# A causal mask moved from TensorE into masked copies for 12 of 32 head pairs, a smaller ring of x, and a new plan

## The chip, the cores and the metric

The kernel runs on one core of a Trainium2 chip. The core has a matrix engine (TensorE, PE in the profile, with its weight loads as PEld), a vector engine (VectorE, DVE), a scalar engine (ScalarE, ACT), GpSimd (POOL) and a sync engine that issues DMAs (SyncE, SP). Each engine runs its own instructions in the order in which they were issued, and they meet through semaphores. The metric is the time of one execution on the device in microseconds; less is better. A time is the median of several runs.

## The reference

A forgetting attention is followed by a SwiGLU block. There are 8 batches of 8 heads with 576 positions of width 64; the model width is 512, the inner width 1536, and 8 x 576 = 4608 tokens go through the second part.

```python
scores = scale * np.matmul(q, k.transpose(0, 1, 3, 2))
cum = np.cumsum(np.log(np.clip(f, 0.0001, 1.0)), axis=-1)
decay = cum[:, :, :, None] - cum[:, :, None, :]
causal = np.triu(np.ones((S, S), dtype=bool), k=1)
scores = np.where(causal, -1000000000.0, scores + decay)
attn = softmax(scores)            # rows, with 1e-9 added to the sum
x = np.matmul(attn, v)            # heads laid side by side: 4608 x 512
g = x @ w_gate
out = (g * sigmoid(g) * (x @ w_val)) @ w_out
```

Within a row of scores the term of the row's own position is the same for every column, so the softmax needs only the gate sums `cum` of the columns.

## The kernel before

**Attention.** Two heads of one batch make a pair, so there are 32 pairs. A row block `i` is 64 positions of both heads (128 partitions) and has 64(i+1) columns. Blocks 0 to 3 are group 0 of a pair, blocks 4 to 8 group 1; each group is a unit, named `a<pair>.<group>` in the table of nudges. For a block TensorE multiplies q (`qz`, negated and scaled) by k (`kt`) into a score bank `sp` (L594). VectorE adds the gate sums `cb` and takes the least value of each row in the same instruction (`tensor_tensor_reduce`, L622; it gives `t` and the least value `tm`). ScalarE takes the exponential and the row's sum (L642). VectorE makes the reciprocals (`lr`, L658 and L660), GpSimd scales the rows into bf16 (`pk`, L678), and the result is transposed into `pT`: on TensorE with a copy by VectorE or ScalarE for pairs 0 to 7 (L708, L713), by a DMA from SyncE's queue (L691) for the rest. TensorE multiplies `pT` by v (`vt`) into a bank `tx` (L734), which is copied into `xT` (L758).

**The mask.** Because the scores are negated, a masked position must be large. In the kernel before, each block's diagonal 64 columns get a second matmul, identity times a 64-column mask, added into the same bank (L598), for every pair below `MFROM`, which is 32: all of them. The other way is in the code but unused. There a copy of a pair's gate sums with the mask added to every 64-column stretch (`copies`, tile `cm`) is used for the diagonal columns, a block is split into a body that adds `cb` and a diagonal that adds `cm`, both parts give their own least value, and a tiny GpSimd instruction (`least`) takes the smaller of the two before the exponential.

**Feed-forward.** `xT` is a ring of `NRING` tokens. For each token tile (`TILES`: 256, 256, seven of 512, 256, 128, 128) TensorE makes gate and value into `gv` banks (L816), ScalarE a tanh (L822), VectorE the products (L824, L827, giving `hh`). TensorE then multiplies by the third weight (L844), and the copy `ot` is stored. This work fills TensorE between pieces of attention.

**What sets the order.** The program describes each operation with its engines, estimated durations, tiles and a priority, and a planner (`Plan.order`) simulates the engines and emits each engine's instructions in the order of its simulated start times. Among operations that could start at the same time the lower priority number goes first. `NUDGE` adds a number to the priority of a unit (`a` attention, `q` its inputs, `v` the cast of v, `f` a feed-forward tile, `o` its output). `STARTUP` is the order of the first loads: `p` is k and q of a pair (first halves for pairs 0 to 3), `k` and `q` the second halves, `c` a pair's gate sums, `v` v, `wg`, `wv`, `wo` weight pieces, `f9` the gates f. Each load in this line is planned behind the one `AHEAD` places before, and a weight load, which GpSimd issues, also behind the one `BEHIND` places before. The gate sums are computed once, stored to a DRAM tensor (L382) and loaded back for each pair, spread over 64 partitions (L513, L430).

Of the kernel before, what the change touches and what calls it, by code (L numbers as in the profile page):

```python
# [8 lines left out]
F32 = mybir.dt.float32  # L9
# [23 lines left out]
class Plan:  # L33
# [29 lines left out]
    def order(self):  # L63
# [72 lines left out]
        while ready:  # L136
# [63 lines left out]
def kernel(  # L200
# [28 lines left out]
    NRING = 2560  # L229
# [10 lines left out]
    MFROM = 32  # L240
# [15 lines left out]
    BEHIND = 6  # L256
# [4 lines left out]
    SLACK = 400  # L261
# [3 lines left out]
    STARTUP = "p0 f9 k0 p2 wv0 wg0 c0 v01 q1 q0 wv2 wg2 c1 v02 v00 k2 v04 c3 q2 wv4 v03 wg4 q3 c2 p4 v11 c4 wg8 wv8 c5 v14 p5 v13 v12 p6 c7 v10 c6 wo0 wo4 wo8 p7"  # L265
# [3 lines left out]
    NUDGE = "a5.0:-2 a8.0:1 a13.0:-1 a15.0:-2 a17.0:-2 a18.0:1.5 a22.0:2.5 a23.0:-1 a25.1:-1 a26.1:-1.5 f1:-2 f5:9 f7:0.5 o3:-4.5 o4:-0.5 o6:-8 o7:-3 q8:-2 q13:-3.5 q20:-2 q23:2 q25:4 q26:3.5 q30:-2"  # L269
# [33 lines left out]
    bufs("t", [P, S], F32, 4)  # L303
    for i in range(0, NB, 2):
        bufs(f"e{i}", [P, QB * (i + 2)], F32, 2)
# [187 lines left out]
    def load_parts(p):  # L493
        b, hp = divmod(p, NPB)
        pl.key(("cb", p), "cb", p)
        for name, x, a, z, r, n in parts(p):
            fk = (name + "f", p, x)
            pl.key(fk, name + "f")
            m = (z - a) // r

            def load(e, fk=fk, src=(k if name == "k" else q), a=a, z=z, r=r, n=n, m=m):
                for u in range(n):
                    h0 = 2 * (hp + u)
                    (nc.scalar if e == "ACT" else nc.sync).dma_start(
                        out=pl.buf(fk)[m * u:m * u + m, :, 0:r * D],
                        in_=src[b, h0:h0 + 2, a:z].rearrange("h (p r) d -> p h (r d)", r=r))
            loads[name, p, x] = pl.op({"ACT" if p == 0 and x == "A" else "SP": 550 * n}, load, (), [fk], -99 + 3 * p, dma=n * (z - a) * 2)
# [367 lines left out]
    for x in STARTUP.split():  # L875
# [96 lines left out]
```

## Time and profile before

| | |
|---|---|
| median of 3 runs | 419.31 us (417.72 to 420.36) |
| span of the profiled execution | 417.2 us |
| DMA, mean over the span | 172 GB/s, 71.83 MB |
| mask matmuls (L598) | 288, mean 197 ns each, as the profile counts |
| weight loads of the identity for them | 288, mean 100 ns |
| mean granted TensorE clock | 0.996 |

A line of the profile names an engine, the source line, and the tiles it writes and reads. "Busy" counts overlapping instructions of one engine once; a matmul's duration reaches from its start to its modelled end, so matmuls that follow each other overlap. The chain of waits is read from the end backwards: each piece is there because the next one waited for it. In a windows view each row is a stretch of the span: its start and end, its length, then busy time and number of instructions for each engine, the granted clock, the DMA engines' busy share and GB/s. In a view of groups a row gives a line, engine, operation and shapes, the count, the busy time and the mean ns, and what the engine waited for before it.

### The profile page before, as it was taken

The numbers are of one execution on the slowest core, as the hardware profiler recorded it, in microseconds if no ns is written. First come the engines' busy times: TensorE is split into PE (matmuls) and PEld (weight loads), VectorE is DVE, ScalarE is ACT, GpSimd is POOL, SyncE is SP. The second block draws the span as 40 slices with busy tenths as digits, with TensorE's granted clock in tenths as the row PEclk, the third lists the DMA queues.
The fourth block names the chain that finished last, engine by engine and source line by source line (L and its number), as shares of the span: only waits on it lengthen the run. The fifth ranks groups of instructions, "written<-read, shape, count | busy, mean of one in ns | idle before, by whom it ended". The sixth has DMA issues, their size and how long they took to land.

```text
span 417.2 us, 9955 instructions
## 1 busy us (share of the span) xinstructions
PE 398.3 (95%) x3250; PEld 232.3 (56%) x3296; DVE 328.9 (79%) x1065; ACT 310.3 (74%) x872; POOL 251.7 (60%) x459
## 2 busy tenths in 40 slices
PE   1979999999999999999999999999999999999996
PEld 0636878665555555555555554555555444457675
DVE  5688999999998899989897797798967764565232
ACT  4798999989995999899999984798996533232221
POOL 7589698987887897976968678267773400000000
PEclk9998999999999999999999999999999999999999
DMA  9999979695999999899999999848999211000211
GB/s 183 253 210 225 190 135 252 159 234 141 200 229 215 264 218 236 203 232 222 228 234 218 240 221 223 194 116 190 221 217 186 55 37 50 25 27 25 77 52 52
DMA packets 144004, 71.83 MB, mean 172 GB/s; under 512 B 117904, under 2 KB 131728, under 8 KB 143952
## 3 DMA queue, kind: packets, MB, share of 16 engines
q1 hardware_dynamic: 137568, 65.95, 71.1%
q0 software_dynamic: 5808, 4.72, 7.6%
q10 hardware_dynamic: 576, 0.52, 0.5%
q8 instruction: 26, 0.43, 0.4%
q14 instruction: 26, 0.21, 0.3%
HBM read 46.65 MB, written 9.58 MB: 135 GB/s over the span
## 4 chain that ended last, share of the span: by engine, by line
PE 86%; DVE 4%; issue 1%; ACT 0%
PE gv L816 43%; PE gv L844 22%; PE sp L594 9%; PE tx L734 6%; PE tx L467 3%; PE sp L598 2%; PE gv L708 2%; DVE t L622 1%; DVE pT L713 1%; DVE hh L827 1%; DVE th L824 1%; DVE qz L481 1%; DVE kt L481 0%; ACT ot L851 0%; DVE tm L622 0%
## 5 line engine op out<-in xcount | busy, mean ns | idle before, releaser
L622 DVE CUSTOM_DVE_ANT_0 t<-sp,cb 128x320 f32<-128x320 f32 (+7 forms) x288 | 130.4, 475 | 12.1 <-PE sp L598 8.6
L678 POOL TENSOR_SCALAR pk<-e,lr 128x128 bf16<-128x128 f32 (+3 forms) x190 | 100.5, 533 | 61.8 <-DVE lr L660 16.5
L816 PE MATMUL gv<-xT,wg 128*128 128x512 bf16 (+2 forms) x563 | 110.6, 327 | 0.8
L816 PE MATMUL gv<-xT,wv 128*128 128x512 bf16 (+2 forms) x562 | 109.3, 324 | 0.9
L844 PE MATMUL gv<-wo,hh 128*128 128x512 bf16 (+1 forms) x425 | 104.2, 373 | 0.8
L824 DVE SCALAR_TENSOR_TENSOR th<-th,gv 128x512 f32<-128x512 f32 x108 | 73.9, 684 | 39.3 <-ACT th L822 38.3
L822 ACT ACTIVATE th<-gv 128x512 f32<-128x512 f32 x108 | 64.1, 594 | 44.0 <-PE gv L816 43.1
L642 ACT ACTIVATE e<-t,tm 128x576 f32<-128x576 f32 (+4 forms) x160 | 88.7, 556 | 8.9 <-DVE tm L622 8.3
L827 DVE TENSOR_TENSOR hh<-th,gv 128x512 bf16<-128x512 f32 x108 | 73.7, 685 | 8.7 <-PE gv L816 4.9
L642 ACT ACTIVATE eo<-t,tm 128x128 f32<-128x128 f32 (+3 forms) x128 | 71.1, 556 | 4.7 <-DVE tm L622 2.9
L594 PE MATMUL sp<-kt,qz 128*128 128x448 bf16 (+6 forms) x320 | 71.9, 293 | 1.5 <-DVE tm L622 1.4
L678 POOL TENSOR_SCALAR pk<-eo,lr 128x128 bf16<-128x128 f32 (+3 forms) x127 | 67.6, 532 | 5.4 <-DVE lr L660 3.1
L816 PEld LDWEIGHTS <-wg 128*128 128x128 bf16 x576 | 49.8, 98 | 35.7
L816 PEld LDWEIGHTS <-wv 128*128 128x128 bf16 x576 | 48.9, 98 | 33.7 <-issue 0.3
L844 PEld LDWEIGHTS <-hh 128*128 128x128 bf16 x444 | 39.9, 98 | 39.0
L598 PE MATMUL sp<-mask,ident 128*128 128x64 bf16 x288 | 48.0, 197 | 0.0
L594 PEld LDWEIGHTS <-qz 128*128 128x128 bf16 x320 | 30.9, 100 | 20.9 <-DVE tm L622 0.9
L851 ACT ACTIVATE ot<-gv 128x512 f32<-128x512 f32 (+1 forms) x31 | 17.9, 580 | 27.1 <-PE gv L844 26.2
L598 PEld LDWEIGHTS <-ident 128*128 128x128 bf16 x288 | 27.2, 100 | 12.6 <-issue 1.9
L734 PE MATMUL tx<-pT,vt 128*64 128x320 bf16 (+4 forms) x448 | 29.6, 266 | 1.9 <-DVE pT L713 1.3
L451 POOL TENSOR_SCALAR qb<-qf 72x1024 bf16<-72x1024 f32 x28 | 29.1, 1041 | 3.1 <-DMA qf<-in_q_dram 2.0
L642 ACT ACTIVATION_READ_ACCUMULATOR e<-t,tm 128x1 f32 x160 | 30.6, 192 | 0.0
(69 smaller groups left out, 389.0 us busy)
## 6 DMA issues: line engine op xcount, KB each, us to landing
out_dram<-ot SPq DMA_DIRECT2D x35, 256.0 KB
vf<-in_v_dram SPq DMA_DIRECT2D x32, 256.0 KB
cb<-cum_f SPq DMA_DIRECT2D x56, 144.0 KB
kf<-in_k_dram SPq DMA_DIRECT2D x28, 288.0 KB
qf<-in_q_dram SPq DMA_DIRECT2D x28, 288.0 KB
wo<-in_moe_w_out_dram POOLq DMA_DIRECT2D x3, 512.0 KB, 10.8
vf<-in_v_dram SPq DMA_DIRECT2D x8, 128.0 KB
wv<-in_moe_w_val_dram POOLq DMA_DIRECT2D x2, 512.0 KB, 8.4
```

The costliest lines, as they stand in the source:

```text
L451: eng[e].tensor_scalar(dst, src, -scale, 1.0, op0=ALU.mult, op1=ALU.mult)
L594: nc.tensor.matmul(sp[:, o:o + z - a], qz[:, i, :, :].rearrange("p h r -> p (h r)"), kt[:, a:z], start=True, stop=not last or p >= MFROM)
L598: nc.tensor.matmul(sp[:, o - QB:o], ident, mask, start=False, stop=True)
L622: nc.vector.tensor_tensor_reduce(out=pl.buf(tk)[:, a:z], in0=pl.buf(sk)[:, o:o + z - a], in1=pl.buf(("cm", p))[:, i, :] if own else pl.buf ...
L642: nc.scalar.activation(pl.buf(ek)[:, :L], pl.buf(tk)[:, :L], AF.Exp, bias=pl.buf(("tm", p, g))[:, 0, i:i + 1], scale=-1.0, accum_out=pl.bu ...
L678: eng[e].tensor_scalar(dst, src, r, 1.0, op0=ALU.mult, op1=ALU.mult)
L734: nc.tensor.matmul(xo[r, 0:QB * n], vt[:, c, 2 * hp + h, :], pT[:, a:a + n, 64 * h:64 * h + 64], start=(c == 0), stop=(c == nch - 1))
L816: nc.tensor.matmul(pl.buf(bk)[:, j * n:j * n + n], wt[:, ko, fc * P:fc * P + P], xT[:, ko, x0:x0 + n], start=ko == 0, stop=ko == KD - 1)
L822: pl.op({"ACT": 487}, lambda e, u=u: nc.scalar.activation(pl.buf(("th", t, u)), pl.buf(("wg", t, u)), AF.Tanh, scale=0.5), [("wg", t, u)], ...
L824: pl.op({"DVE": 605}, lambda e, u=u: nc.vector.scalar_tensor_tensor(pl.buf(("th", t, u)), pl.buf(("th", t, u)), 1.0, pl.buf(("wg", t, u)), ...
L827: pl.op({"DVE": 605}, lambda e, u=u: nc.vector.tensor_mul(pl.buf(("hh", t, u)), pl.buf(("th", t, u)), pl.buf(("wv", t, u))), [("u", t, u), ...
L844: nc.tensor.matmul(pl.buf(bk)[:, 0:z - a], hh[:, (fc % nf) * n + ms * P:(fc % nf) * n + ms * P + P], wo[:, fc, a:z], start=fc == 0, stop=f ...
```

## The change

Pairs 20 to 31 use the masked copies (`MFROM` 32 to 20, with two `cm` tiles of 128 x 576 f32), pairs 0 to 19 keep the mask matmul. The ring of x shrinks from 2560 to 2048 tokens. The first loads of k and q, of which some were two DMAs planned as one operation, become one operation each. The planner's times for a load's beginning and end are other numbers, its slack goes from 400 to 950 and `BEHIND` from 6 to 4, and the order of the first loads and the nudges of the units are new.

```diff
             if o.dma:
                 q = e == "POOL"
-                at = max(wire[q], s + (2550 if q else 2000))
+                head, tail = (2850, 500) if q else (1500, 1000) if s < 12000 else (2000, 1100)
+                at = max(wire[q], s + head)
...
-                o.end = wire[q] + 1100
+                o.end = wire[q] + tail
...
-    NRING = 2560
+    NRING = 2048
...
-    MFROM = 32
+    MFROM = 20
...
-    BEHIND = 6
+    BEHIND = 4
...
-    SLACK = 400
+    SLACK = 950
...
-    STARTUP = "p0 f9 k0 p2 wv0 wg0 c0 v01 q1 q0 wv2 wg2 c1 v02 v00 k2 v04 c3 q2 wv4 v03 wg4 q3 c2 p4 v11 c4 wg8 wv8 c5 v14 p5 v13 v12 p6 c7 v10 c6 wo0 wo4 wo8 p7"
+    STARTUP = "f9 p0 wv0 p2 q0 wg2 k0 q1 wg0 c1 v02 k2 q3 wv4 wv2 c0 v00 v01 q2 v03 wg4 c2 c3 p4 wg8 c6 c4 v04 wv8 c5 c7 p5 v11 p6 v14 wo4 v13 wo0 v10 wo8 v12 p7"
...
-    NUDGE = "a5.0:-2 a8.0:1 a13.0:-1 a15.0:-2 a17.0:-2 a18.0:1.5 a22.0:2.5 a23.0:-1 a25.1:-1 a26.1:-1.5 f1:-2 f5:9 f7:0.5 o3:-4.5 o4:-0.5 o6:-8 o7:-3 q8:-2 q13:-3.5 q20:-2 q23:2 q25:4 q26:3.5 q30:-2"
+    NUDGE = "a0.0:-4 a1.0:-30 ... a29.1:23 a30.1:17 a31.0:34.5 a31.1:19.5 ... f0:-978.5 f1:3 f10:16.5 ... q31:37.5 ... v0:53.5 ..."
...
+    bufs("cm", [P, NB, QB], F32, 2)
...
-            def load(e, fk=fk, src=(k if name == "k" else q), a=a, z=z, r=r, n=n, m=m):
-                for u in range(n):
-                    h0 = 2 * (hp + u)
-                    (nc.scalar if e == "ACT" else nc.sync).dma_start(
-                        out=pl.buf(fk)[m * u:m * u + m, :, 0:r * D],
-                        in_=src[b, h0:h0 + 2, a:z].rearrange("h (p r) d -> p h (r d)", r=r))
-            loads[name, p, x] = pl.op({"ACT" if p == 0 and x == "A" else "SP": 550 * n}, load, (), [fk], -99 + 3 * p, dma=n * (z - a) * 2)
+            def load(e, u, fk=fk, src=(k if name == "k" else q), a=a, z=z, r=r, m=m):
+                h0 = 2 * (hp + u)
+                (nc.scalar if e == "ACT" else nc.sync).dma_start(
+                    out=pl.buf(fk)[m * u:m * u + m, :, 0:r * D],
+                    in_=src[b, h0:h0 + 2, a:z].rearrange("h (p r) d -> p h (r d)", r=r))
+            loads[name, p, x] = [pl.op({"ACT": 720} if p == 0 and x == "A" else {"SP": 620}, lambda e, u=u, load=load: load(e, u),
+                                       (), [fk], -99 + 3 * p, dma=(z - a) * 2.35) for u in range(n)]
...
-            line += [loads["k", n, "A"], loads["q", n, "A"]]
+            line += loads["k", n, "A"] + loads["q", n, "A"]
...
-            line.append(loads[x[0], n, "B"])
+            line += loads[x[0], n, "B"]
```

The table of nudges after has some 110 entries; the marks " ... " in it stand for those not shown. The code that `MFROM` switches on stands in the kernel above: `copies`, and in `scores` the cuts, the two least values and `least`. With 2048 tokens the ring's seam falls inside a unit (`spread`, `cut`) at tokens 2048 and 4096, so that its copy into `xT` is made in two pieces.

More of the change, by code (lines that the diff above doesn't have):

```diff
@@ L264 @@
     CBACK = 5
-    STARTUP = "p0 f9 k0 p2 wv0 wg0 c0 v01 q1 q0 wv2 wg2 c1 v02 v00 k2 v04 c3 q2 wv4 v03 wg4 q3 c2 p4 v11 c4 wg8 wv8 c5 v14 p5 v13 v12 p6 c7 v10 c6 wo0 wo4 wo8 p7"
+    STARTUP = "f9 p0 wv0 p2 q0 wg2 k0 q1 wg0 c1 v02 k2 q3 wv4 wv2 c0 v00 v01 q2 v03 wg4 c2 c3 p4 wg8 c6 c4 v04 wv8 c5 c7 p5 v11 p6 v14 wo4 v13 wo0 v10 wo8 v12 p7"
     HEAD = "00 10 20 30 11 01 31 21"
-    NUDGE = "a5.0:-2 a8.0:1 a13.0:-1 a15.0:-2 a17.0:-2 a18.0:1.5 a22.0:2.5 a23.0:-1 a25.1:-1 a26.1:-1.5 f1:-2 f5:9 f7:0.5 o3:-4.5 o4:-0.5 o6:-8 o7:-3 q8:-2 q13:-3.5 q20:-2 q23:2 q25:4 q26:3.5 q30:-2"
+    NUDGE = "a0.0:-4 a1.0:-30 a1.1:0.5 a10.0:-3 a10.1:-1 a11.1:1 a12.0:-1.5 a12.1:0.5 a13.0:-2 a13.1:-1 a14.0:-1.5 a14.1:-2 a15.0:1 a15.1:-0.5 a17.0:-1 a18.1:5.5 a19.0:-1.5 a19.1:1 a2.0:0.5 a2.1:-1.5 a20.0:3 a20.1:2 a21.0:2 a21.1:2.5 a22.0:0.5 a22.1:2 a23.0:2.5 a24.0:4 a24.1:7 a25.1:-0.5 a26.0:-1 a26.1:2 a27.1:2.5 a28.0:0.5 a28.1:4 a29.0:4 a29.1:23 a30.1:17 a31.0:34.5 a31.1:19.5 a4.1:1 a5.0:-1 a5.1:-0.5 a6.1:-2 a7.1:-3 a8.0:-0.5 a9.0:-2.5 f0:-978.5 f1:3 f10:16.5 f11:4 f2:5 f3:0.5 f4:-1 f5:-6.5 f7:-0.5 f9:-2 o0:2 o1:4 o10:-11.5 o11:-3 o4:-0.5 o5:-1.5 o6:-9 o7:-1.5 o8:2.5 o9:2 q1:-1.5 q10:0.5 q11:3.5 q12:2.5 q13:3.5 q14:2 q15:1 q16:-0.5 q17:-3 q19:-6.5 q2:-0.5 q20:0.5 q21:-1.5 q22:4 q23:-1 q25:1.5 q28:9.5 q29:-2 q3:1.5 q30:5.5 q31:37.5 q4:1 q6:-1 q8:3 q9:1.5 v0:53.5 v1:3.5 v2:7 v3:4 v4:-0.5 v5:7.5 v6:1"
     WAIT = ""
```

## Prediction

> **What bounds the kernel now.** I read the page first: the span, the busy shares, the slices and the chain that ended last.
>
> ```profile
> span 417.2 us, 9955 instructions
> PE 398.3 (95%) x3250; PEld 232.3 (56%) x3296; DVE 328.9 (79%) x1065; ACT 310.3 (74%) x872; POOL 251.7 (60%) x459
> PE   1979999999999999999999999999999999999996
> PEclk9998999999999999999999999999999999999999
> ...
> PE 86%; DVE 4%; issue 1%; ACT 0%
> PE gv L816 43%; PE gv L844 22%; PE sp L594 9%; PE tx L734 6%; PE tx L467 3%; PE sp L598 2%; PE gv L708 2%; DVE t L622 1%; DVE pT L713 1%; DVE hh L827 1%; DVE th L824 1%; DVE qz L481 1%; DVE kt L481 0%; ACT ot L851 0%; DVE tm L622 0%
> ```
>
> TensorE is busy in all but the first and last slices, and 86% of the chain is TensorE. Since a busy TensorE need not be at its peak, I then asked for the busy time by stage. I cut at 22.7 us (first weighted sum with v), 34.3 us (first gate matmul), 193 us (about where pair 20 begins, by the count of score matmuls, ten a pair) and 334 us (the last attention work).
>
> ```profile
> core 0: us, PE busy (x) PEld busy (x) DVE busy (x) ACT busy (x) POOL busy (x), PEclk, DMA share, GB/s
> 0.00:10.00 10.00, 0.87 (x5) 0.64 (x6) 5.26 (x13) 4.69 (x7) 7.43 (x33) 1.00 0.90 182
> 10.00:22.70 12.70, 12.68 (x79) 8.31 (x78) 8.70 (x42) 9.93 (x38) 8.20 (x17) 1.00 1.18 250
> 22.70:34.30 11.60, 7.81 (x68) 4.19 (x69) 10.39 (x43) 10.72 (x34) 9.85 (x19) 0.95 1.04 211
> 34.30:193.00 158.70, 157.39 (x1478) 98.18 (x1496) 147.93 (x511) 145.11 (x415) 129.63 (x221) 0.99 0.98 207
> 193.00:334.00 141.00, 139.99 (x1053) 73.19 (x1070) 117.80 (x404) 115.25 (x340) 96.58 (x173) 1.00 0.93 199
> 334.00:417.20 83.20, 79.54 (x574) 47.80 (x580) 38.81 (x57) 24.65 (x43) 0.00 (x0) 1.00 0.13 43
> ```
>
> From 34.3 to 334 us TensorE is idle for only 1.3 + 1.0 us. Its idle time lies at the start: 9.1 us before 10 us and 3.8 us in 22.7 to 34.3. The 3.7 us after 334 are mostly the last copy and store, which the diff leaves alone. So there are two places to gain: TensorE work that goes away after 34.3 us, and an earlier or fuller start. From pair 20 on the other engines have room: VectorE 141.0 - 117.8 = 23.2 us, GpSimd 141.0 - 96.6 = 44.4 us.
>
> **Part 1, the mask leaves TensorE.** Pairs 20 to 31 lose nine mask matmuls each, 12 x 9 = 108 of 288. Their price is the advance along the chain, not the busy figure, because matmuls overlap.
>
> ```profile
> by line: PE gv L816 43.2%; PE gv L844 22.1%; PE sp L594 8.9%; PE tx L734 5.6%; PE tx L467 3.3%; PE sp L598 1.8%; PE gv L708 1.6%; issue 1.1%; DVE t L622 1.0%; DVE pT L713 0.6%; DVE hh L827 0.6%; DVE th L824 0.6%; DVE qz L481 0.5%; DVE kt L4
> ...
> 229.52 0.08 PE sp L594
> 229.60 0.03 PE sp L598
> 229.63 0.03 PE sp L594
> 229.66 0.03 PE sp L598
> ...
> L598 PEld LDWEIGHTS <-ident 128*128 128x128 bf16 x288 | 27.2, 100 | 12.6 <-issue 1.9
> ```
>
> 1.8% of 417.2 us is 7.5 us, or 26 ns for each of 288; the single rows say 0.03. So 108 x 26 ns = 2.8 us leave a saturated engine. The 100 ns load of the identity before each mask is hidden: two rows follow each other after 0.03 us.
>
> The Trainium skill, "TensorE: Matmul & The Clock Gate", section Back-to-back issue gap, puts a sustained stream of weight load and matmul pairs at about 81 ns a matmul for 128 columns. By that figure the 108 would be worth 8.7 us. The rows disagree, and the rows decide.
>
> **Part 2, what takes its place.** A pair now needs one copy of its gate sums with the mask added (128x576 f32, on GpSimd or VectorE), seven score blocks split into a body and a 64-column diagonal, and eight tiny GpSimd minima. Each exponential (L642, ScalarE) then waits for GpSimd's minimum instead of VectorE's own. The trace has none of these, so neighbours bound them.
>
> ```profile
> 20.26 0.33 DVE L622 CUSTOM_DVE_ANT_0 t<-sp,cb 128x192 f32<-128x192 f32 x1
> 20.51 0.22 DVE L622 CUSTOM_DVE_ANT_0 t<-sp,cb 128x64 f32<-128x64 f32 x1
> 20.65 0.29 DVE L622 CUSTOM_DVE_ANT_0 t<-sp,cb 128x128 f32<-128x128 f32 x1
> ...
> L827 DVE TENSOR_TENSOR hh<-th,gv 128x512 bf16<-128x512 f32 x108 | 73.7, 685 | 8.7 <-PE gv L816 4.9 <-PE gv L844 0.2
> L678 POOL TENSOR_SCALAR pk<-e,lr 128x512 bf16<-128x512 f32 x64 | 44.3, 692 | 61.8 <-DVE lr L660 16.5 <-DVE tm L622 14.2 <-ACT th L822 13.3
> L678 POOL TENSOR_SCALAR pk<-eo,lr 128x128 bf16<-128x128 f32 x32 | 11.9, 372 | 0.0
> L351 POOL MEMSET ls<- 128x9 f32 x6 | 0.4, 105 | 0.1
> ```
>
> Splits: start to start, 192 columns take 0.25 us and 64 take 0.14, so 0.86 ns a column and 0.085 us fixed; by busy time the fixed part is 0.22 - 0.055 = 0.165. The 84 splits add 7.1 to 13.9 us of VectorE; I take 7.1, since the next sum starts in that distance. Copies: on VectorE 0.685 x 576/512 = 0.77 us, 9.2 us in all. On GpSimd between one pass, 0.78, and two for two inputs, 1.56: 9.4 to 18.7 us. I take the middle, 14, having no row nearer. Minima: between the small memset, 0.105, and the 128-column scaling, 0.372; the scaling's line through 128 and 512 columns meets zero columns at 0.265, and I take that as the same kind of operation. 96 x 0.265 = 25.4 us (10.1 to 35.7).
>
> VectorE: 7.1 to 13.9, plus at most 9.2 for copies, is under its 23.2 free. GpSimd: 14 + 25.4 = 39.4 of 44.4 free, with 19.5 and 54.4 as ends. So both hide, GpSimd narrowly, and it is also idle after 334 us, where the plan may put work. What hides them is feed-forward work on TensorE that is already fed. If that cover goes, behind a late copy stand on VectorE the sums and the gating (L824, L827) that free the gv banks; behind a late minimum stand on ScalarE the tanh (L822) and the next exponentials. TensorE then waits on a bank. I book 0, with the ends below as rivals.
>
> **Part 3, the ring.** With 2048 tokens a write of x waits for the gate of the token 2048 before. How far x runs ahead is read from the gate matmuls and from the writes of x, the same stretch in two answers (L816 columns: TensorE, weight load; L758: VectorE, ScalarE).
>
> ```profile
> 334.00:417.20 83.20, 51.05 (x409) 32.13 (x410) 1.00 0.13 43
> sum 417.20, PE 207.48 PEld 98.37; mean PE 34.58 PEld 16.40
> ...
> 334.00:417.20 83.20, 0.00 (x0) 0.70 (x2) 1.00 0.13 43
> ```
>
> At 334 us all but two writes of x are done while 51.05/207.48 of the gates, some 1130 tokens, are left, a gap well under 2048. The ring costs no wait. It does cut eight copies of x in two, at 2048 and 4096 tokens: eight short instructions over ScalarE and VectorE, inside the room above; 0.
>
> **Part 4, the start.** The first loads keep their number and issues; only their places change. The plan's load times (head, tail) are numbers that move order, no work.
>
> ```profile
> 4.83 0.60 SPq L774 DMA_DIRECT2D vf<-in_v_dram  x1
> 9.62 0.49 SPq L382 DMA_DIRECT2D cum_f<-t  x1
> 9.97 0.60 POOL L778 CAST vt<-vf 128x512 bf16<-128x512 f32 x1
> 15.86 1.22 SPq L513 DMA_DIRECT2D cb<-cum_f  x2
> ...
> 28.64 0.56 DVE L713 COPY pT<-gv 128x768 bf16<-128x768 bf16 x1 [0.61 <-PE gv L708]
> 31.97 0.49 DVE L561 COPY qz<-tx 64x320 bf16<-64x320 bf16 x1
> 32.52 0.36 PE L734 MATMUL tx<-pT,vt 128*64 128x256 bf16 x4 [0.20 <-DVE qz L561]
> 34.30 1.91 PE L816 MATMUL gv<-xT,wg 128*128 128x256 bf16 x8
> 36.48 1.04 PE L816 MATMUL gv<-xT,wv 128*128 128x256 bf16 x8
> ```
>
> The first gate needs x of pairs 0 to 3. Pair 3's weights were in place at 28.64 + 0.56 = 29.2 us, but its product with v ran at 32.52, behind other scores and a tx bank that VectorE freed late: 3.3 us. After the gaps the clock fell (0.95 for this stretch), and the first eight gate matmuls took 1.91 against 1.04 us, 0.9 more. Tile 0's gates now rank with the first pairs (f0 -978.5), so at most 4.2 us can go. Against it: a first row of gate sums (c1), which must wait for the stored sums, is issued on SyncE ahead of k2, q3 and both v blocks of the first product. Sixteen issues at 0.6 us put v at 14 to 17 us; a load took 9.97 - 4.83 = 5.1 us to its cast, so v is ready at 19 to 22, just before 22.7. A weight block put behind another on GpSimd's queue lands long before 30 us. I take half, -2.0 us, between -4.2 and +1.
>
> **Sum.** 417.2 - 2.8 - 2.0 = 412.4 us of span. The three runs had a median of 419.3 (417.7 to 420.4), 2.1 above the profiled span, so I forecast **414.5 us**, 1.1% faster.
>
> **Rivals.**
> - Only the masks go, and the start stays: 419.3 - 2.8 = 416.5. For it: ScalarE and VectorE are already busy 10.7 and 10.4 of 11.6 us before the first gate.
> - The whole start gain comes: 419.3 - 2.8 - 4.2 = 412.3. For it: nothing but order stands between 29.2 and 32.5 us.
> - The identity's loads were not hidden: 108 x 0.1 = 10.8, less 2.0 for the start, 406.5. The 0.03 us rows speak against it.
> - GpSimd becomes the bound from pair 20 on: the minima queue behind 0.69 us scalings, ScalarE waits, and TensorE stalls in its fixed order. It decides when copies and minima pass 44.4 us; at the upper end, 54.4, it adds 10 us: 419.3 - 2.8 + 10 = 426.5. Against it: room after 334 us and some 1130 tokens of lead. The Trainium skill, "GPSIMD Engine Reference", section Engine selection, calls a two-input elementwise operation about twice as slow there as on VectorE; no run here shows it yet.
> - The new plan does not run as planned, and its own stalls eat the masks: 419.3 or a little over.
>
> **How the numbers follow.** About 1% is what a measurement of this kernel can tell from no change. Forecast 0.46 (0.29 past 1%, 0.17 within, as the bound is at 415.1); masks alone 0.18 (0.02 past); whole start 0.14; loads 0.02; GpSimd 0.17 (0.15 slower, 0.02 within); plan 0.03 (0.02 within, 0.01 slower). Faster 0.47, same 0.37, slower 0.16. The range 410.5 to 421 leaves out the loads, a little of the whole start (together 0.05) and most of the GpSimd case (0.14). The faster and unchanged cases alone span 411 to 418.
>
> **What would show it.** Right: 180 mask matmuls instead of 288; the first gate between 30 and 33 us; TensorE's idle time from the first gate to the end of attention still under 3 us; GpSimd above 90% busy in the stage of pairs 20 to 31. Wrong: exponentials that wait for GpSimd minima with TensorE gaps behind them, writes of x that wait for gates, or a first gate later than 34.3 us.

## The result, and the profile after

| | before | after |
|---|---|---|
| median, runs of this comparison | 419.56 us (417.72 to 420.36, 4 runs) | 424.33 us (422.94 to 424.95, 4 runs) |
| span of the profiled execution | 417.2 us | 423.1 us |
| mask matmuls | 288 | 180 |

The changed kernel is slower: the ratio is 1.0121, with a 95% interval of 1.0085 to 1.0157. I had forecast 414.5 us, with 421 as the upper end. The page of the changed kernel, the lines that answer to those shown of before:

```profile
span 423.1 us, 9963 instructions
PE 399.1 (94%) x3140; PEld 230.2 (54%) x3188; DVE 337.7 (80%) x1231; ACT 311.9 (74%) x885; POOL 288.8 (68%) x564
...
PE   3969996999999999999999999999999999999996
PEclk9988998999999999999999999999999999999999
...
PE 62%; POOL 15%; DMA 7%; DVE 6%; ACT 4%; issue 4%; SPq 0%; another core or an unknown queue 0%; POOLq 0%; ACTq 0%
```

TensorE was 86% of the chain of waits and is now 62%; GpSimd holds 15% and loads 7%. The slices of 10.6 us show a 6 at the seventh place, from about 63 to 74 us. Two windows views, before and then after, cut into the same stages (start and end, length, busy time and instructions of TensorE, its weight loads, VectorE, ScalarE and GpSimd, then the granted clock, the share of the DMA engines and GB/s):

```profile
0.00:40.00 40.00, 27.07 (x202) 17.70 (x203) 28.85 (x111) 29.76 (x87) 31.18 (x76) 0.96 1.06 218
40.00:80.00 40.00, 39.66 (x490) 32.33 (x490) 39.83 (x127) 37.92 (x104) 32.68 (x52) 1.00 0.93 194
80.00:200.00 120.00, 118.98 (x1001) 65.27 (x1018) 110.37 (x400) 109.64 (x327) 97.59 (x171) 1.00 1.00 214
200.00:340.00 140.00, 138.99 (x1026) 72.09 (x1044) 115.53 (x382) 110.86 (x319) 90.24 (x163) 1.00 0.89 189
```

```profile
0.00:40.00 40.00, 28.61 (x214) 18.30 (x217) 32.18 (x122) 31.87 (x95) 31.46 (x76) 0.91 1.04 203
40.00:80.00 40.00, 35.23 (x400) 28.36 (x400) 32.41 (x99) 31.61 (x83) 29.78 (x49) 0.96 1.01 196
80.00:200.00 120.00, 118.52 (x1029) 66.87 (x1047) 109.34 (x385) 106.36 (x326) 97.07 (x168) 1.00 1.01 212
200.00:340.00 140.00, 137.25 (x920) 68.77 (x937) 124.73 (x556) 115.02 (x330) 124.61 (x260) 1.00 0.85 184
```

Up to 40 us little differs in TensorE's work (202 against 214 instructions). From 40 to 80 us it was busy 39.66 us and is now busy 35.23, with 400 instructions instead of 490: 4.4 us are lost there, and VectorE falls from 39.83 to 32.41 as well, so more than TensorE alone was held up. From 200 to 340 us, where the masked copies are, its idle time goes from 1.0 to 2.75 us. Some matmul records are missing in both traces, so both are upper bounds; the experiments narrow them.

What TensorE ran around the hole, and what GpSimd ran (start, length, then in brackets the idle time before it and what ended that); both are timelines of the changed kernel:

```profile
64.28 1.04 PE L818 MATMUL gv<-xT,wv 128*128 128x256 bf16 x8
65.16 0.22 PE L710 MATMUL gv<-ident,pk 128*128 128x128 bf16 x1
67.23 0.23 PE L710 MATMUL gv<-ident,pk 128*128 128x128 bf16 x1 [1.85 <-POOL pk L680]
...
70.40 1.90 PE L818 MATMUL gv<-xT,wg 128*128 128x256 bf16 x8
```

```profile
52.86 0.80 POOL L797 DMA_DIRECT2D wo<-in_moe_w_out_dram  x1
...
54.21 0.74 POOL L797 DMA_DIRECT2D wo<-in_moe_w_out_dram  x1
...
59.63 1.04 POOL L680 TENSOR_SCALAR pk<-e,lr 128x512 bf16<-128x512 f32 x2 [0.50 <-DVE lr L662]
65.90 0.61 POOL L780 CAST vt<-vf 128x512 bf16<-128x512 f32 x1 [5.22 <-DMA vf<-in_v_dram]
66.48 0.69 POOL L680 TENSOR_SCALAR pk<-eo,lr 128x512 bf16<-128x512 f32 x1
```

GpSimd stands at the cast of a block of v from 60.7 to 65.9 us. Behind it in its order are the scalings (`pk`) that TensorE must transpose, so TensorE gets no more than single transposes from 65.4 us on; and when it resumes in full at about 70 us, eight gate matmuls take 1.90 us where they took 1.04. The chain of waits leads to the load:

```profile
51.10 1.04 POOL qb L453
52.16 0.31 SPq L425
...
52.53 0.63 SPq L776
53.20 12.64 DMA vf<-in_v_dram
...
65.90 0.61 POOL vt L780
```

SyncE itself could not issue this v load before 52.5 us: ahead of it in SyncE's order stood a load of q whose buffer a GpSimd cast (`qb`) freed only at 52.14. (SyncE had issued nothing since 44.4 us.) Then the load took 12.6 us, beside two `wo` loads issued at 52.9 and 54.2 and four more loads of v and k that SyncE issued by 57.7 us. In the forecast's row for the start a v load had taken 5.1 us to its cast.

For the second stage, the groups of the new instructions, as answers on a tile and on a line give them (durations as least, median and most in ns), and the row of the masks:

```profile
L579 POOL TENSOR_TENSOR cm<-cb,maskf x7: 1391/1409/1421, 197.7 to 324.3; 128x576 f32<-128x576 f32 x7
L579 DVE TENSOR_TENSOR cm<-cb,maskf x5: 768/876/2083, 227.1 to 312.0; 128x576 f32<-128x576 f32 x5
```

```profile
L635 POOL TENSOR_SCALAR tm<-tm x96: 269/279/770, 210.6 to 342.4; 128x1 f32<-128x1 f32 x96
...
  ACT eo L644: 9.2, 10
  ACT e L644: 5.6, 11
```

```profile
L600 PE MATMUL sp<-mask,ident 128*128 128x64 bf16 x180 | 30.7, 201 | 0.1
```

The 96 least values take 279 ns at the median, near the 265 I took; ScalarE waits 9.2 + 5.6 = 14.8 us for them. Where TensorE's time is held up in that stage is seen in the chain of waits from 200 to 340 us, by line, before and after:

```profile
by line: PE gv L816 51.3%; PE gv L844 23.4%; PE sp L594 10.6%; PE tx L734 8.1%; PE tx L467 3.7%; PE sp L598 2.2%; issue 0.7%
```

```profile
by line: POOL pk L680 21.7%; PE gv L818 15.8%; issue 8.2%; PE gv L846 7.9%; POOL tm L635 7.5%; PE sp L596 4.1%; DVE t L624 3.9%; ACT e L644 3.5%; DVE th L826 3.1%; PE tx L736 2.9%; POOL kb L455 2.8%; DVE hh L829 2.4%; POOL vt L780 2.2%; ACT
```

Before, this chain is all matmuls but for 0.7% of issue. After, GpSimd's scalings are 21.7% and its least values 7.5%.

The granted clock alone does not explain the slower time: one of the changed kernel's four runs had a mean granted clock of 1.000 and took 422.94 us, still above every run of before (417.72 to 420.36).

### The profile page after: what moved, and what is told of

Its sections match the earlier page's. It is cut to its first block, busy times and chain, and to the rows that moved or that the text cites. A ratio compares the mean times of both kernels' runs of the same rounds, so it can differ in the third digit from the quotient of the medians.

```text
span 423.1 us, 9963 instructions
## 1 busy us (share of the span) xinstructions
PE 399.1 (94%) x3140; PEld 230.2 (54%) x3188; DVE 337.7 (80%) x1231; ACT 311.9 (74%) x885; POOL 288.8 (68%) x564
## 4 chain that ended last, share of the span: by engine, by line
PE 62%; POOL 15%; DMA 7%; DVE 6%; ACT 4%; issue 4%; SPq 0%; another core or an unknown queue 0%; POOLq 0%; ACTq 0%
PE gv L818 30%; PE gv L846 16%; POOL pk L680 9%; PE sp L596 6%; PE tx L736 5%; DMA vf<-in_v_dram 3%; POOL tm L635 2%; PE gv L710 2%; DVE t L624 2%; PE tx L469 2%; DMA qf<-in_q_dram 1%; ACT e L644 1%; DMA cum_f<-t 1%; DVE th L826 1%; POOL kb L455 1%
## 5 line engine op out<-in xcount | busy, mean ns | idle before, releaser
L624 DVE CUSTOM_DVE_ANT_0 t<-sp,cb 128x320 f32<-128x320 f32 (+7 forms) x276 | 124.6, 465 | 16.9 <-ACT eo L644 9.1
L680 POOL TENSOR_SCALAR pk<-e,lr 128x128 bf16<-128x128 f32 (+3 forms) x191 | 101.6, 535 | 25.1 <-DVE lr L662 9.3
L846 PE MATMUL gv<-wo,hh 128*128 128x512 bf16 (+1 forms) x421 | 101.4, 373 | 1.2 <-issue 0.2
L644 ACT ACTIVATE e<-t,tm 128x64 f32<-128x64 f32 (+4 forms) x160 | 88.6, 555 | 9.9 <-POOL tm L635 5.6
L644 ACT ACTIVATE eo<-t,tm 128x512 f32<-128x512 f32 (+3 forms) x128 | 71.2, 557 | 20.1 <-POOL tm L635 9.2
L596 PE MATMUL sp<-kt,qz 128*128 128x512 bf16 (+7 forms) x315 | 72.5, 295 | 4.1 <-DVE tm L624 2.0
L680 POOL TENSOR_SCALAR pk<-eo,lr 128x384 bf16<-128x384 f32 (+2 forms) x127 | 68.6, 540 | 5.9 <-ACT e L644 2.5
L635 POOL TENSOR_SCALAR tm<-tm 128x1 f32<-128x1 f32 x96 | 26.6, 283 | 11.3 <-DVE tm L624 10.5
L624 DVE DVE_READ_ACCUMULATOR2_ANT tm<- 128x1 f32 x404 | 33.2, 82 | 0.0
L600 PE MATMUL sp<-mask,ident 128*128 128x64 bf16 x180 | 30.7, 201 | 0.1
```

Source lines behind the costliest of these rows:

```text
L596: nc.tensor.matmul(sp[:, o:o + z - a], qz[:, i, :, :].rearrange("p h r -> p (h r)"), kt[:, a:z], start=True, stop=not last or p >= MFROM)
L600: nc.tensor.matmul(sp[:, o - QB:o], ident, mask, start=False, stop=True)
L624: nc.vector.tensor_tensor_reduce(out=pl.buf(tk)[:, a:z], in0=pl.buf(sk)[:, o:o + z - a], in1=pl.buf(("cm", p))[:, i, :] if own else pl.buf ...
L635: eng[e].tensor_scalar(m[:, 0, :], m[:, 1, :], m[:, 0, :], None, op0=ALU.min)
L644: nc.scalar.activation(pl.buf(ek)[:, :L], pl.buf(tk)[:, :L], AF.Exp, bias=pl.buf(("tm", p, g))[:, 0, i:i + 1], scale=-1.0, accum_out=pl.bu ...
L680: eng[e].tensor_scalar(dst, src, r, 1.0, op0=ALU.mult, op1=ALU.mult)
```

## The experiments

Three questions: which half of the change costs what, whether the hole after 40 us is one bad wait or a property of the new start, and which part of the new start makes it. "Busy" below is TensorE's busy time in the 40 us from 40 to 80 us (39.66 before, 35.23 after). The kernel before was run beside each group, with medians from 418.35 to 419.16 us; ratios are to those.

| run | median us | ratio to before, 95% | busy, 40 to 80 us |
|---|---|---|---|
| e1 cast later | 422.91 | 1.0098, 1.0067 to 1.0130 | 37.27 |
| e2 wo later | 424.34 | 1.0134, 1.0099 to 1.0169 | 36.24 |
| e3 minima on VectorE | 423.53 | 1.0113, 1.0074 to 1.0151 | 36.41 |
| e4 mask back on TensorE | 424.19 | 1.0127, 1.0093 to 1.0161 | 36.13 |
| e5 new start alone | 425.92 | 1.0195, 1.0164 to 1.0227 | 36.99 |
| e6 masks, old start | 423.24 | 1.0114, 1.0080 to 1.0148 | 39.66 |
| e7 masks, old order | 434.44 | 1.0390, 1.0366 to 1.0414 | 39.60 |
| e8 no wo loads | 422.04 | 1.0067, 1.0037 to 1.0098 | 36.82 |
| e9 old load order | 427.89 | 1.0226, 1.0172 to 1.0280 | 35.55 |
| e10 old early nudges | 423.25 | 1.0116, 1.0067 to 1.0166 | 38.60 |
| e11 old load times | 430.10 | 1.0279, 1.0239 to 1.0319 | 35.74 |
| e12 ring alone | 419.27 | 1.0022, 0.9998 to 1.0045 | 39.71 |
| e13 old v nudges | 433.29 | 1.0346, 1.0311 to 1.0381 | 37.42 |
| e14 old v and feed-forward nudges | 429.31 | 1.0246, 1.0205 to 1.0287 | 36.05 |
| e15 old pair nudges | 428.51 | 1.0249, 1.0195 to 1.0303 | 34.80 |
| e16 e10 without copies | 423.01 | 1.0102, 1.0076 to 1.0129 | 38.48 |

**The halves.** e5 keeps all that is new but the masked copies and the shorter ring, and plans anew:

```diff
-    NRING = 2048
+    NRING = 2560
-    MFROM = 20
+    MFROM = 32
-    bufs("cm", [P, NB, QB], F32, 2)
```

> The changed kernel without the masked copies and with the ring of 2560 tokens: the new first loads, load times, slack, order and nudges alone. Its planned order is the changed kernel's up to about 144 us. Theory C (the loss of 5 us lies before 80 us, in the new start, and the masked copies break even): 423 to 425. Rival D (the copies or the ring cost what was lost): 419.

It took 425.92 us, 1.6 to 2.3% over the kernel before, a little above the range that I had given, and no less than the changed kernel. So the new start with its plan costs at least as much as the whole change does. (Its late nudges were found together with the copies, so part of the 6.9 us may be theirs.) The shortage from 40 to 80 us is there without any copy:

```profile
40.00:80.00 40.00, 36.99 (x415) 29.47 (x418) 33.26 (x100) 32.78 (x86) 30.76 (x51) 0.91 1.04 202
```

e6 is the other half: the kernel before with the copies and the short ring, the old first loads and early nudges, and the new nudges of the late units, which the copies need.

```diff
-    NRING = 2560
+    NRING = 2048
-    MFROM = 32
+    MFROM = 20
+    bufs("cm", [P, NB, QB], F32, 2)
-    NUDGE = "a5.0:-2 a8.0:1 ..."
+    NUDGE = "a5.0:-2 a8.0:1 ... a20.0:3 a20.1:2 ..."
```

> The kernel before with the masked copies of pairs 20 to 31 and the ring of 2048 tokens, its own first loads, load times, slack and nudges, and the changed kernel's nudges for the late units alone (pairs from 20 on, feed-forward tiles from 5 on, v from batch 5 on). Its planned order is that of the kernel before up to 149 us. Theory C: no start loss, copies that break even, 418 to 421 against some 419.3 before. Rival D: 422 or more.

It took 423.24 us, so the copies did not break even here, against the theory. TensorE is as busy from 40 to 80 us as before (39.66); the loss lies mainly from 200 to 340, as its window and the chain by line there show:

```profile
200.00:340.00 140.00, 133.92 (x891) 67.03 (x907) 123.64 (x540) 111.07 (x320) 116.95 (x248) 1.00 0.89 183
```

```profile
by line: PE gv L817 20.3%; POOL pk L679 16.9%; POOL tm L634 6.0%; ACT eo L643 5.2%; PE gv L845 5.1%; DMA pT<-pk 4.6%; DMA qf<-in_q_dram 4.6%; issue 3.9%; POOL qb L452 3.6%; PE sp L595 3.4%; DVE cm L578 3.3%; DVE t L623 3.1%; ACT th L823 3.1
```

TensorE is idle there for up to 140 - 133.92 = 6.1 us, and the chain runs over GpSimd's scalings and least values. Here the late nudges stand in another plan than the one they were found for, so this is not the price of the copies in the changed kernel. That price is measured by e4, which keeps the changed kernel's order of every engine, puts the 108 masks back on TensorE and leaves out copies, splits and least values:

```diff
     def copies(p):
+            return
...
-                                     start=True, stop=not last or p >= MFROM)
+                                     start=True, stop=not last)
-                    if last and p < MFROM:
+                    if last:
...
+                    if p >= MFROM and 0 < i < 8:
+                        if last:
+                            return
+                        z, last = z + QB, True
+                    own, two = False, two and i < 8
```

> The order of the changed kernel, with the mask of pairs 20 to 31 put back on TensorE: no copies, no split sums, no minima, 108 mask matmuls more. Its output is the reference's. TensorE gains 108 x 26 ns = 2.8 us of work. Theory B (what takes the mask's place costs about 2.5 us): about 424.5, no different from the changed kernel. Rival (what takes its place is hidden, and the mask's 2.8 us are a pure gain): 427.

It took 424.19 us against 424.33, and its stage from 200 to 340 us, in the windows view and in the chain by line, reads:

```profile
200.00:340.00 140.00, 140.00 (x1046) 72.15 (x1045) 115.71 (x390) 114.81 (x330) 91.34 (x161) 1.00 0.88 187
```

```profile
by line: PE gv L824 49.8%; PE gv L852 24.7%; PE sp L597 12.1%; PE tx L742 7.5%; PE tx L469 3.7%; PE sp L601 2.4%
```

TensorE has no idle time there, and the chain is all matmuls. (The changed kernel's own order has 140 - 138.31 = 1.7 us of it, by the row of e1 below, which differs from it only at one cast of the start and lacks no record.) So the copies win the masks' time, which I put at 2.8 us, and lose about the same. Each of the two ratios to before has an interval of 0.35% to either side, so by the times "about the same" holds to some 2 us. The work done in the stage is a closer measure. Add up the columns that the matmuls stream there, by the shapes in the traces of e1 and e4, which lack no matmul record: apart from the masks TensorE got through 337,792 columns in e1, with the copies, and 337,536 in e4, without them. Only 1.7 us of the loss shows as idle time.

e3 moves the 96 least values from GpSimd to VectorE in the changed kernel's order:

```diff
-                        eng[e].tensor_scalar(m[:, 0, :], m[:, 1, :], m[:, 0, :], None, op0=ALU.min)
+                        nc.vector.tensor_scalar(m[:, 0, :], m[:, 1, :], m[:, 0, :], None, op0=ALU.min)
```

> The order of the changed kernel, with the 96 minima of pairs 20 to 31 issued on VectorE at the same places of the order instead of GpSimd. Theory B (the exponentials wait for GpSimd's minima, 283 ns each and queued, and this costs the 2.5 us by which TensorE falls behind between 200 and 310 us): about 422 against 424.3, and the waits of ScalarE for the minima (14.8 us) go. Rival (these waits are hidden by the lead of feed-forward work): 424 to 425, the added VectorE work (96 short instructions) costing up to 1.

423.53 us: no change that can be told, and TensorE got through 337,408 columns other than masks from 200 to 340 us, the same again. ScalarE's waits stay, only with another releaser (us in total, times, longest):

```profile
ACT eo L644 <- DVE tm L635: 7.9, 10, 1.9
ACT e L644 <- DVE tm L635: 7.4, 15, 1.2
```

15.3 us in place of 14.8. So the waits are not tied to GpSimd; one more step stands between the sums and the exponential, and its engine has other work in front of it, whichever engine it is.

e7 asks what the copies cost in an order that was never planned for them: the old order of every engine, with the copies put on GpSimd three microseconds ahead of their pair's sums, the splits and least values on VectorE, and the short ring. In it a pair's copy may replace that of two pairs earlier before its last blocks have read it, so part of the masked values are not the reference's; the instructions are the same.

```diff
+        order = sorted(order + [Copy(p) for p in range(20, NPAIR)], key=lambda o: o.start)
...
+                        if last and i:
+                            nc.vector.tensor_scalar(tm[:, 0, i:i + 1], tm[:, 1, i:i + 1], tm[:, 0, i:i + 1], None, op0=ALU.min)
```

> The kernel before with its whole planned order kept, the mask matmuls of pairs 20 to 31 taken out, and in their places the split sums, the minima (on VectorE, straight behind the sums) and the copies (on GpSimd, 3 us ahead of the pair's first sum); x in a ring of 2048 tokens. Nothing is planned anew. If the 2.8 us of masks were a pure gain: 416.5. Theory C (break even, by waits of TensorE on late sums): 419 to 420. If VectorE cannot take the splits and minima without making TensorE wait: 421 or more.

434.44 us. The start is untouched (39.60 us busy), and the late stage falls apart, with TensorE waiting for score banks that VectorE frees late (its window, then TensorE's waits by what was waited for: us in total, times, longest):

```profile
200.00:340.00 140.00, 127.65 (x834) 61.97 (x850) 125.25 (x620) 105.69 (x304) 100.64 (x164) 1.00 0.85 183
```

```profile
PE sp L596 <- DVE tm L628: 9.8, 23, 1.1
```

So the extra work of VectorE and GpSimd is not hidden merely because TensorE has other work: in this order, which left no room for it, it was not.

e12 is the short ring alone, on the old order of every engine; a write of x that crosses the ring's end becomes two.

```diff
-    xT = sb.tile([P, KD, NRING], BF16)
+    RING = 2048
+    xT = sb.tile([P, KD, RING], BF16)
```

> The kernel before with nothing but the ring of x cut to 2048 tokens in memory; the order of every engine is the old one and nothing is planned again, and a write of x that crosses the end of the ring is two instructions. My forecast took the ring at nothing: within 0.3% of the kernel before, 418.5 to 420.5 us, and no write of x that waits for a gate matmul for over 1 us in all. Rival (the shorter ring holds writes of x back): 421 us or more, with such waits.

419.27 us, a ratio of 0.9998 to 1.0045. Where an engine was idle before an instruction on `xT`, it was the product with v (`tx`) that ended the wait, and never a gate matmul:

```profile
  PE tx L735: 12.1, 18
```

**One bad wait?** e1 moves the one cast of v that GpSimd stood at behind the scalings that wait behind it:

```diff
+        x = made(("vt", 1, 3))
+        order.remove(x)
+        order.insert(order.index(made(("vt", 1, 0))), x)
```

> The order of the changed kernel, with one instruction moved: GpSimd's cast of the v block that landed at 65.8 us stands behind the ten scalings it had held up, not before them. The load itself is left where it is. Theory A (GpSimd waits in order for a late v block, and TensorE's gap of 60 to 80 us is all due to that): the lost time of that stretch, some 5 us by the clock and the gap, comes back, so about 419 against 424.3 of the changed kernel. Rival (the gap only shows a lag of the whole attention chain, and another wait takes its place): 423 or more.

422.91 us, all but the rival's 423, and GpSimd no longer stands from 60.7 to 65.9. But GpSimd's timeline then shows the next two waits for loads, 1.1 us for a k and 2.7 us for the next block of v, and behind them some of the transposes on TensorE stand until 75.3 us:

```profile
67.02 0.82 POOL L455 CAST kb<-kf 96x768 bf16<-96x768 f32 x1 [1.12 <-DMA kf<-in_k_dram]
...
72.14 0.61 POOL L780 CAST vt<-vf 128x512 bf16<-128x512 f32 x1 [2.74 <-DMA vf<-in_v_dram]
```

Its late stage, used above:

```profile
200.00:340.00 140.00, 138.31 (x939) 68.79 (x938) 124.72 (x556) 114.96 (x330) 124.62 (x260) 1.00 0.86 186
```

e2 issues the two `wo` loads after that cast, so that they don't share the DMA engines with the v load:

```diff
+        for k in (("wo", 0), ("wo", 4)):
+            x = made(k)
+            order.remove(x)
+            order.insert(order.index(made(("vt", 1, 3))) + 1, x)
```

> The order of the changed kernel, with the issues of the two w_out blocks (512 KB each) that stood before the late v block's cast on GpSimd put right behind that cast. Theory A with its cause in the DMA engines (the w_out blocks, issued within 1.4 us of the v block, share the engines with it and stretch its 12.6 us): the v block lands 5 to 7 us after its issue, GpSimd's wait of 5.2 us is under 1, and the time is about 419. Rival (the v block was slow for another reason, such as the other loads of SyncE's queue): the wait stays over 3 us and the time over 422.

424.34 us. The cast finds its data, though it comes only at 64.08 us, so this does not tell how much sooner the load landed. Other loads are late in its place: TensorE waits for a `wv` piece and GpSimd for a q, as the view of its waits from 40 to 80 us has it.

```profile
POOL qb L453 <- DMA qf<-in_q_dram: 3.0, 1, 3.0
...
PE gv L818 <- DMA wv<-in_moe_w_val_dram: 2.5, 1, 2.5
```

e8 cuts the `wo` loads to a 32nd of their bytes; the output projection then multiplies by the gate weights, so its result isn't the reference's, with the same matmuls.

```diff
-                out=wo[:, c:c + 4, :], in_=moe_w_out[c * P:(c + 4) * P, :]...
+                out=wo[:, c:c + 4, 0:16], in_=moe_w_out[c * P:(c + 4) * P, 0:16]...
```

> The changed kernel with the three w_out loads cut to 1/32 of their columns and the projection reading the gate weights in their place; so the projection's result is left wrong and its work is the same. Theory C1 (the new start loses because transfers come bunched and late through full DMA engines, so that relief of 3 MB of reads between 50 and 75 us brings it back): 419 to 421, and no wait of GpSimd on a v block. Rival C2 (the start loses by its order on the engines, not by the DMA engines): 423 or more.

422.04 us, 2.3 us under the changed kernel (its ten runs reach from 418.73 to 424.36), and 36.82 us busy instead of 35.23. GpSimd no longer waits for a v block. So the traffic is probably a part of it, but its size is uncertain: the intervals of the two ratios overlap, and e3 and e4, whose order up to 80 us is the changed kernel's own, were busy for 36.41 and 36.13 us. The three loads of 512 KB are 1.5 MB, of some 16 MB that move by 80 us (203 and 196 GB/s over 40 us each). Most of the shortage is left when it is gone.

What is left in e8 is nearly all one wait, and it shows a second late load. GpSimd issues the last `wv` piece too, in its own order; in turn, the issue before, the issue in the changed kernel, and TensorE's wait in e8 and in e14 (below):

```profile
39.27 0.79 POOL L791 DMA_DIRECT2D wv<-in_moe_w_val_dram  x1
```

```profile
44.54 0.80 POOL L793 DMA_DIRECT2D wv<-in_moe_w_val_dram  x1
```

```profile
55.93 1.05 PE L818 MATMUL gv<-xT,wv 128*128 128x256 bf16 x8 [3.02 <-DMA wv<-in_moe_w_val_dram]
```

```profile
54.91 1.05 PE L818 MATMUL gv<-xT,wv 128*128 128x256 bf16 x8 [3.53 <-DMA wv<-in_moe_w_val_dram]
```

Over all traces the two go together. Where this issue comes by 41 us (before, e6, e7, e9 to e12, e16), TensorE shows no wait for the piece; where it comes at 42.4 to 47.0 us (the changed kernel, e1 to e5, e8, e13 to e15), TensorE waits 0.8 to 3.5 us for it, but for e1. In the changed kernel the issue stands behind scalings that GpSimd could begin only at 41.1 us. It is not the whole shortage, since e9 and e11 below issue it early and are short by other waits.

**Which part of the new start?** Three runs each put one part back as before and plan all units anew. e9 takes the written order of first loads and the look-back:

```diff
-    BEHIND = 4
+    BEHIND = 6
-    STARTUP = "f9 p0 wv0 p2 q0 wg2 k0 q1 ..."
+    STARTUP = "p0 f9 k0 p2 wv0 wg0 c0 v01 q1 ..."
```

> The changed kernel with the written list of first loads and the look-back of the planner put back as before; the masked copies, the ring of 2048 tokens, the new nudges, slack and load times stay; all units are planned again. TensorE is busy 35.23 of the 40 us from 40 to 80 us in the changed kernel and 39.66 before. Theory (the order of the first loads brings on the shortage after 40 us): at least 38.5 us busy in that stretch, and 419 to 421 us. Rival (the nudges that place the early casts, scalings and transposes bring it on, whatever order the loads have): under 37.5 us busy, and 423 to 426 us. Both expect the waits for GpSimd's minima from 200 to 340 us to stay.

427.89 us and 35.55 us busy. The theory fell: with the old order of loads the shortage stays, and the time is above both ranges that I had given. e10 puts back the nudges of the early units (pairs and their q and k below 12, feed-forward tiles and v tiles below 3):

```diff
-    NUDGE = "a0.0:-4 a1.0:-30 ... f0:-978.5 f1:3 ... v0:53.5 v1:3.5 v2:7 ..."
+    NUDGE = "a5.0:-2 a8.0:1 f1:-2 q8:-2 ..."
```

> The changed kernel with the nudges of the first twelve pairs, of the first feed-forward tiles and of the first three v tiles put back as before; the new order of first loads, look-back, slack and load times stay, and the masked copies too; all units are planned again. Theory (the order of the first loads): TensorE stays under 37.5 of 40 us busy from 40 to 80 us, 422 to 425 us. Rival (the nudges): at least 38.5 us busy, 419 to 421 us. If this and the run with the old list both stay under 37.5, neither alone brings the shortage on, and what they share, the plan's load times, is next.

```profile
40.00:80.00 40.00, 38.60 (x468) 31.23 (x469) 39.29 (x126) 36.64 (x99) 31.10 (x51) 1.00 0.98 194
200.00:340.00 140.00, 137.40 (x912) 67.50 (x910) 120.64 (x538) 113.56 (x327) 119.89 (x252) 1.00 0.87 179
```

38.60 us busy, as the rival had it, though the time, 423.25 us, isn't the 419 to 421 that I expected with it: 1.4 us of idle time are left in this stage, and 2.6 stand from 200 to 340 us, where the copies are. e11 puts back the load times that the planner reckons with:

```diff
-                head, tail = (2850, 500) if q else (1500, 1000) if s < 12000 else (2000, 1100)
+                head, tail = (2550, 1100) if q else (2000, 1100)
```

> The changed kernel with the planner's load times (the time from an issue to the wire and from the wire to its use) put back as before; all else stays as changed, and all units are planned again. Theory (the order of the first loads, whatever times the plan believes): TensorE under 37.5 of 40 us busy from 40 to 80 us, 422 to 426 us. Rival (the new times, which take a load for quicker than it lands there, let the plan put casts ahead of the data): at least 38.5 us busy, 419 to 421 us.

430.10 us and 35.74 us busy: putting the load times back does not end the shortage either, and the time is again above both. The next three put back one group of the early nudges at a time.

> The changed kernel with the nudges of the first three v tiles alone put back as before (v0 had 53.5, which holds its casts back); all units are planned again. Theory (the late v casts, for which GpSimd waits in its order, bring on the shortage): TensorE at least 38.5 of 40 us busy from 40 to 80 us, 421 to 424 us. Rival (no single nudge does; the pairs and q loads placed anew draw the loads into a bunch): under 37.5 us busy, 423 to 428 us.

> The changed kernel with the nudges of the first three v tiles and of the first feed-forward gates and projections put back as before; those of the pairs and q loads stay new; all units are planned again. Theory (v casts, or tile 0's gates ranked before all else): at least 38.5 of 40 us busy from 40 to 80 us, 421 to 424 us. Rival (pairs and q loads): under 37.5 us busy, 423 to 428 us.

> The changed kernel with the nudges of the first twelve pairs and of the first q loads put back as before; those of the v tiles and of the feed-forward tiles stay new; all units are planned again. Theory (v casts or tile 0's gates): under 37.5 of 40 us busy from 40 to 80 us, 423 to 428 us. Rival (pairs and q loads): at least 38.5 us busy, 421 to 424 us.

37.42, 36.05 and 34.80 us busy, and 433.29, 429.31 and 428.51 us, all above the times that I had given. Every mixture has the shortage: the new pair and q nudges have it with the old ones of v and feed-forward (e14), and the new ones of v and feed-forward have it with the old ones of the pairs (e15). So no single group can be named, neither mine nor the rival's. A mixture is a third plan, and its numbers were not found together. What e13 gains from 40 to 80 us it loses later:

```profile
80.00:200.00 120.00, 116.75 (x986) 65.13 (x1001) 103.36 (x377) 107.04 (x324) 94.14 (x165) 0.97 0.98 206
```

TensorE was idle there for 1.0 us before and 1.5 after, and is here for 3.3. Last, e16 is e10 with the copies taken out (masks on TensorE, ring of 2560 tokens):

> The run with all old early nudges, with the masked copies taken out as well: the causal mask of pairs 20 to 31 is a matmul again, the ring has 2560 tokens, and the new order of first loads and the new load times stay; all units are planned again. If the copies hold what that run had over the kernel before (3.7 us more lost on TensorE from 200 to 340 us, against 2.8 us of masks saved): 418 to 421 us, and TensorE at least 38.5 of 40 us busy from 40 to 80 us. If the new order of first loads and load times hold it: 422 to 425 us.

423.01 us, and 38.48 us busy, just under the bound that I had set. It is no faster than e10 with the copies, so once more no gain or loss from the copies can be told. The time is inside the range for the new order of first loads and load times; but the profiled execution, the fastest of nine, had a span of only 418.8 us, while the nine runs reach from 420.59 to 425.68. What makes this kernel vary by 5 us stays open.

## Why the prediction was wrong, step by step

**The step that failed** is Part 4: "The first loads keep their number and issues; only their places change." From it came "I take half, -2.0 us, between -4.2 and +1." I priced the new start by one event, the first gate matmul. I took it that what comes after 34.3 us would stay fed, as in the trace of before. The new start alone (e5) costs 6.9 us against the median of its runs of before, and the changed kernel's order without the copies (e4) 5.0. The cost lies from 40 to 80 us, where I had booked nothing. Two traces that lack no matmul record, e12 (the order of before) and e4 (the changed order), give its size in columns streamed: up to 40 us e4 is ahead by 1,920, and from 40 to 80 us it gets through 81,344 against 95,040. At the 345,984 columns that e12 gets through from 200 to 340 us, the 13,696 that are missing are worth 5.5 us. That is more than the busy time shows, since part of the busy time ran at a lower clock. In the row of before this stage has 0.3 us of idle time, and the DMA engines are busy for 0.93 of it: that it was both full and tight was in a view that I could have asked for. A plan made anew places casts, scalings and issues against loads of which one took 5.1 us at the start and another 12.6 here. The cast of v that stood before its data held up all that was behind it on GpSimd, and the `wv` piece that GpSimd issued late held up TensorE.

Of the cause of that hole the runs settle this much. It isn't the copies (e4, e5) or the ring (e12), nor one misplaced cast alone (e1). Putting back the order of the first loads (e9) or the load times (e11) by itself does not end it. Part of it is probably the bytes that compete (e8; 0.4 to 1.6 us of busy time, by which of the runs in the same order it is held against). It goes with the early nudges as a whole: e10, whose trace lacks no record either, gets through 92,288 columns from 40 to 80 us, 4.4 of the 5.5 us. Which of them, and why the mixtures are worse still, stays open (e13 to e15). The new slack and the split of the first loads into one operation each were not put back by themselves; e10 keeps both and is short by the last 1.1 us.

**The first gate.** I expected it between 30 and 33 us; it came at 36.54 instead of 34.30, and the first product with v at 31.32 instead of 22.7 us, as the timeline of the changed kernel has them:

```profile
31.32 0.85 PE L736 MATMUL tx<-pT,vt 128*64 128x256 bf16 x8
...
36.54 1.04 PE L818 MATMUL gv<-xT,wg 128*128 128x256 bf16 x8
```

Yet nothing was lost by that: TensorE had done as much by 40 us (214 instructions against 202), since scores and transposes stood in the gap. Those were the wrong marks to judge a start by. Another of my signs did tell: from the first gate to 340 us TensorE was idle for up to 9.0 us in this trace, not under 3.

**Part 1, the masks.** 180 are left, as forecast. The 2.8 us were not measured by themselves; e4 has the 108 masks more to do, in a stage without idle time, and takes no longer.

**Part 2, what takes their place.** The prices were near: the least values 279 ns (265 taken), the copies 1.41 us on GpSimd, inside the bounds of 0.78 to 1.56, and 0.88 on VectorE (0.77 taken), at the median. The Trainium skill, "GPSIMD Engine Reference", section Engine selection, puts a two-input operation at about twice as slow on GpSimd; the ratio of these medians is 1.6, somewhat less, and the measurement decides. What failed is "So both hide, GpSimd narrowly" and "I book 0". I compared sums of busy time with room in a stage, 39.4 of 44.4 us. GpSimd was busy for 34.4 us more than before from 200 to 340 us, 124.6 of 140, so the room sufficed; but the least value is a step in a chain, and what counts is the wait in front of it, 14.8 us on ScalarE. That is the mechanism of my rival with GpSimd as the bound, at a price of about 3 us and not 10; and e3 shows that it isn't tied to GpSimd.

**Part 3, the ring.** Right: e12 lies within 0.45% of before, and no write of x waited for a gate.

**The sum.** The masks' -2.8 stood as it was; what ate it, about as much, stood at 0; and the start, which cost some 5 us, stood at -2.0. The rival "its own stalls eat the masks", 419.3 us with a chance of 0.03, was the nearest in kind. It was too small, and I had given it next to nothing because the planner's order wasn't in the trace of before; what was in it was how little slack that order leaves. The rival on GpSimd, 426.5 us, lies nearest in number, but that is luck: its 10 us were to come from the copies, and most of the loss came from the start.

## What to carry to other kernels

When a change makes a plan anew, price the stage that is full now as something that can be lost, and not only the gap to be won: read how little idle time and how busy a DMA it has, and give the loss the larger chance. Room in a stage hides work only if nobody waits for it; a step put between two engines can cost its wait, however cheap the instruction is. And to tell the parts of such a change apart, keep the order of every engine and swap one part's instructions (e4, e12): runs that were planned anew came out 3 to 9 us above the changed kernel though each put a part of it back (e9, e11, e13 to e15).

## What the hardware showed that I had not expected

A 256 KB load of v took 5.1 us to its cast at the start and 12.6 us to land when issued at 53.2 us beside two 512 KB loads and four more of v and k, with the DMA engines busy all through (a share of 0.90 in the first 10 us before, and of 1.09 from 53.2 to 65.8 us). Behind a hole from 65.4 to 69.8 us, in which TensorE ran only three single matmuls, the eight next gate matmuls took 1.90 us instead of 1.04, and the granted clock of the stage was 0.96 where it had been 1.00. The copies on VectorE took 768 to 2083 ns with a median of 876: one of five took more than twice the usual time, and no run here shows why.
